# Transposing q and k by DMA instead of on TensorE, in an attention kernel with a maxout FFN behind it

## The chip, the cores and the metric

The kernel runs on one core of a Trainium2 chip. The metric is device time in microseconds. A core has the engines TensorE (PE, matmuls; PEld is its weight load), VectorE (DVE), ScalarE (ACT), GpSimd (POOL) and SyncE (SP), each with its own queue of instructions, and 16 DMA engines that they share. SP and POOL start nearly all transfers of this kernel.

## The reference

Two parts, one behind the other. Attention with a relative position bias, over 8 batches, 8 heads, 576 positions and 64 values per head, and then a feed-forward layer with the maximum of three products:

```python
scores = scale * np.matmul(q, k.transpose(0, 1, 3, 2))         # q, k, v: (8, 8, 576, 64) float32
scores = scores + bias.transpose(2, 0, 1)[None, :, :, :]       # bias[i, j, head] = table[bucket(|i - j|), head]
scores = scores - np.max(scores, axis=-1, keepdims=True)
attn = np.exp(scores)
attn = attn / (np.sum(attn, axis=-1, keepdims=True) + 1e-09)
attn_out = np.matmul(attn, v)
x = attn_out.transpose(0, 2, 1, 3).reshape(B * S, H * D)       # (4608, 512)
h = np.maximum(np.maximum(x @ w1, x @ w2), x @ w3)             # w1, w2, w3: (512, 768)
out = h @ w_out                                                # (4608, 512) float32
```

The bias depends on the distance alone, and from 128 on it is constant, so only a band around the diagonal has to be treated.

## The kernel before

The work goes in pairs of heads: `HP = 4` pairs for each of 8 batches. A pair's two heads of 64 values fill the 128 partitions. q and k are loaded with positions on the partitions, converted from float32 to bf16 by the transfer (`load_q`, `load_k`, issued from POOL), but the score product needs the 64 values of a head on the partitions. So each pair's q and k must be transposed.

Positions 0 to 511 are four blocks of 128 (`KT = 4`) in `batch[b][0]` (q) and `batch[b][1]` (k). The last 64 positions of both heads lie in one more block, in `qtail` and `ktail`, each head in its own half of the partitions and of the columns, with zeros elsewhere. A pair has thus five blocks of 128 x 128 for q and five for k.

`transposes(b, hp)` makes them on PE: ten transposes (through `tr`, line 98) into one PSUM tile `tp` of the pool `ps_s`, which has two buffers that the score tiles use as well, and then two copies by DVE (line 365) into the bf16 tiles `qT` and `kT` in SBUF, two buffers each. It is called once per pair, one pair ahead. Batch 0 has a version of its own, `first_transposes`, which works while the loads are still coming in.

For each pair, the main loop (lines 535 to 569) does this:

- `visit(qT, kT, e4, 0)` (line 397): the scores of all 512 keys against queries 0 to 255, eight matmuls into two tiles `sc`, and the exponentials on ACT (line 395);
- `next_late()`: an `attend` of a pair before. It multiplies the exponentials with v (tile `a`), takes the logarithm of the row sums and the reciprocal by ACT (`ld`, `rd`), and leaves the quotients to DVE, which write them into `xT` (line 462);
- `fill(13, ...)`: some FFN work between, in portions of at most 13 units of PE work; hooks inside it place the quotients and `left_keys`, the last 64 keys;
- `visit(qT, kT, e4, 1)`, the next `attend`, the `transposes` for the pair ahead, another `fill(13, ...)` with `left_queries` (tile `scq`) inside.

`times_band` multiplies the exponentials near the diagonal with the exponentiated bias, on DVE. The FFN (`ffn`) works on chunks of 512 rows, whose portions are spread over a batch's eight fills: products `ps` from `xT` and the weights into the pool `ps_f` (two buffers), a copy by ACT (`m0`), two maxima by DVE (`m`, line 296, and `hT`, line 303), then the output product `pso`, a copy to `osb` (line 316, three buffers) and the store by SP (line 320). Two chunks and the rest of the last one are left for the end, behind the last pair.

PE's order is the program's: every matmul and transpose goes through `inorder`, which places an instruction behind all that was written before it for its engine. The other engines' instructions that have no `inorder` are placed by a planner. Loads for batch b + 2 stand in the last pair of batch b, since they write into the buffer from which batch b's transposes read:

```python
if ahead:
    nxt = transposes(*ahead)
if hp == HP - 1 and b + 2 < B:
    batch[b + 2] = load_tiles()
    load_q(b + 2, 0, H)
    load_k(b + 2, 0, H)
```

The functions that the diff touches:

Of the kernel before, what the change touches and what calls it, by code (L numbers as in the profile page):

```python
# [11 lines left out]
BF16 = mybir.dt.bfloat16  # L12
# [27 lines left out]
def kernel(  # L40
# [12 lines left out]
    nc = tc.nc  # L53
    B, H, S, D = q.shape
    d_model, d_ff = moe_w1.shape
    NB = bias_table.shape[0]
    P = 128
    assert d_model == H * D and S == 576 and D == 64 and NB == 32 and H == 8
    inv_sqrt_d = 1.0 / float(np.sqrt(D))
    HP = H // 2  # L60
# [3 lines left out]
    KT = 4  # L64
# [3 lines left out]
    CH = 512  # L68
# [6 lines left out]
    stage = ctx.enter_context(tc.tile_pool(name="stage", bufs=1))  # L75
    loads = ctx.enter_context(tc.tile_pool(name="loads", bufs=2))
    qkt = ctx.enter_context(tc.tile_pool(name="qkt", bufs=2))
    qk0 = ctx.enter_context(tc.tile_pool(name="qk0", bufs=1))
    ep = ctx.enter_context(tc.tile_pool(name="ep", bufs=3))
    nrm = ctx.enter_context(tc.tile_pool(name="nrm", bufs=3))  # L80
    ffnw = ctx.enter_context(tc.tile_pool(name="ffnw", bufs=2))
# [1 line left out]
    ps_s = ctx.enter_context(tc.tile_pool(name="ps_s", bufs=2, space=bass.MemoryType.PSUM))  # L83
# [8 lines left out]
    inorder = tc.keep_in_program_order  # L92
# [4 lines left out]
    def tr(*args):  # L97
        inorder(nc.tensor.transpose(*args))  # L98
# [22 lines left out]
    def dve_copy(out_, in_):  # L121
        inorder(nc.vector.tensor_copy(out_, in_))
# [20 lines left out]
    def load_main(src, b, h0, h1, dst):  # L143
        x = main_part(src, b)
        if h1 - h0 < KT:
            for h in range(h0, h1):
                nc.gpsimd.dma_start(out=dst[:, :, h, :], in_=x[:, :, h, :])
        else:
            for t in range(KT):
                nc.gpsimd.dma_start(out=dst[:, t, h0:h1, :], in_=x[:, t, h0:h1, :])  # L150
# [5 lines left out]
    def load_tail(src, b, h0, h1, dst):  # L156
        for par in range(2):
            nc.gpsimd.dma_start(  # L158
                out=diag(dst[b % 2], par, h0, h1), in_=tail_part(src, b, h0, h1, par)
            )  # L160

    def load_q(b, h0, h1):
        load_main(q, b, h0, h1, batch[b][0])
        load_tail(q, b, h0, h1, qtail)

    def load_k(b, h0, h1):
        load_main(k, b, h0, h1, batch[b][1])
        load_tail(k, b, h0, h1, ktail)

    def load_v(b, h0, h1):  # L170
        load_main(v, b, h0, h1, vx[b % 2][:].rearrange("p t (h c) -> p t h c", c=P)[:, :, :, 0:D])
        load_tail(v, b, h0, h1, vt)
# [14 lines left out]
    def load_tiles():  # L187
        q_sb = loads.tile([P, KT, H, D], BF16, tag="q_sb", name="q_sb")
        k_sb = loads.tile([P, KT, H, D], BF16, tag="k_sb", name="k_sb")
        return q_sb, k_sb  # L190

    batch = [None] * B
    batch[0] = load_tiles()
    load_k32(0, 2, nc.sync)
    for par in range(2):
# [6 lines left out]
    ident = const.tile([P, P], BF16, name="ident")  # L202
# [7 lines left out]
        out=negc[:], in0=tableT[:, NB - 1 : NB], scalar1=-1.0, scalar2=None, op0=ALU.mult,  # L210
# [40 lines left out]
    def make_band(hp):  # L251
        dve_copy(band[hp][:], hank[:, 2 * hp : 2 * hp + 2, ::-1])
        for par in range(2):
            dve_copy(bandt[hp][64 * par : 64 * par + 64, :], band[hp][0:64, par, 0:192])
# [96 lines left out]
            hook()  # L351


    def transposes(b, hp):
        hs = slice(2 * hp, 2 * hp + 2)
        tp = ps_s.tile([P, 2, 2 * CH], BF16, tag="sc", name="tp")
        made = []
        for j, tl in enumerate((qtail, ktail)):
            for t in range(KT):
                tr(tp[:, j, P * t : P * t + P], batch[b][j][:, t, hs, :].rearrange("p h d -> p (h d)"), ident[:])  # L360
            tr(tp[:, j, KT * P : KT * P + P], tl[b % 2][:, hp, :], ident[:])
        for j in range(2):
            name = ("qT", "kT")[j]
            x = qkt.tile([P, (KT + 1) * P], BF16, tag=name, name=name)
            nc.vector.tensor_copy(x[:], tp[:, j, 0 : (KT + 1) * P])  # L365
            made.append(x)
        return made

    def first_transposes(hp):

        hs = slice(2 * hp, 2 * hp + 2)
        tp = [ps_f.tile([P, 2 * CH], BF16, tag="ff", name=n) for n in ("tq", "tk")]
        made = [qk0.tile([P, (KT + 1) * P], BF16, tag=f"{n}{hp}", name=n) for n in ("qT", "kT")]
        for j in range(2):
            for t in range(KT):
                tr(tp[j][:, P * t : P * t + P], batch[0][j][:, t, hs, :].rearrange("p h d -> p (h d)"), ident[:])
            dve_copy(made[j][:, 0 : KT * P], tp[j][:, 0 : KT * P])

        def tails():
            c = slice(KT * P, KT * P + P)  # L380
            for j, tl in enumerate((qtail, ktail)):
                tr(tp[j][:, c], tl[0][:, hp, :], ident[:])
                dve_copy(made[j][:, c], tp[j][:, c])
        return made, tails
# [12 lines left out]
    def visit(qT, kT, e4, c):  # L397


        for tt in range(0, KT, 2):  # L400
            sc = ps_s.tile([P, 2, 2, QS], F32, tag="sc", name="sc")
            for t in range(2):
                for par in range(2):
                    r = slice(64 * par, 64 * par + 64)
                    mm(
                        sc[:, par, t, :], lhsT=kT[r, P * (tt + t) : P * (tt + t) + P],
                        rhs=qT[r, c * QS : c * QS + QS],
                    )
            exp(e4[:, tt : tt + 2, :, c * QS : c * QS + QS].rearrange("p t h q -> p h t q"), sc[:])
# [60 lines left out]
    def next_late():  # L470
        return late.pop(0)() if late else (lambda: None)

    def e_tiles():
        return (
            ep.tile([P, KT, 2, S], BF16, tag="e4", name="e4"), ep.tile([P, S], BF16, tag="et", name="et")
        )
# [18 lines left out]
    for c, (lo, hi) in enumerate(((0, QS), (QS, S))):  # L495
        for hp in range(HP):
            qT, kT = qk[hp]
            e4, et = e_tiles()
            visit(qT, kT, e4, c)
            if c == 0:  # L500
                if hp == 0:
                    first_tail()
                if hp == 1:
                    dve_copy(batch[0][1][:, :, 4:H, :], k32[:, :, 4:H, :])
                if hp + 1 < HP:
                    main, tail = first_transposes(hp + 1)
                    tail()
                    qk.append(main)

            quotients = next_late() if (c, hp) != (1, 1) else (lambda: None)  # L510
            if c == 0:
                make_band(hp)
                if hp == 1:
                    tail_constants(1)
                    batch[1] = load_tiles()
                    load_q(1, 0, H)
                    load_k(1, 0, H)
            for t in range(KT):
                times_band(hp, e4, t, lo, min(hi, QM))
            if c == 1 and hp == 1:  # L520
                load_v(1, 0, H)
                add_ffn(0, QS)
            if c == 1 and hp == HP - 1:
                nxt = transposes(1, 0)
                batch[2] = load_tiles()
                load_q(2, 0, H)
                load_k(2, 0, H)
            fill(
                12, quotients, lambda: left_keys(hp, qT, kT, et, lo, hi),
                *([lambda: left_queries(qT, kT, e4)] if c == 1 else []),  # L530
            )
            times_band(hp, e4, KT - 1, QM, hi)
            late.append(lambda hp=hp, e4=e4, et=et, lo=lo, hi=hi: attend(0, hp, e4, et, lo, hi))

    pairs = [(b, hp) for b in range(1, B) for hp in range(HP)]
    for i, (b, hp) in enumerate(pairs):
        qT, kT = nxt
        ahead = pairs[i + 1] if i + 1 < len(pairs) else None
        e4, et = e_tiles()

        visit(qT, kT, e4, 0)
        quotients = next_late()
        times_band(hp, e4, 0, 0, QS)
        fill(13, quotients, lambda: left_keys(hp, qT, kT, et, 0, S))


        visit(qT, kT, e4, 1)
        quotients = next_late()  # L550
        times_band(hp, e4, 1, 0, QM)
        times_band(hp, e4, 2, 0, QM)
        if hp == 0:
            if b + 1 < B:
                load_v(b + 1, 0, H)
            if b == 1:
                quotients()
                quotients = lambda: None
            add_ffn(*((QS, QS) if b == 1 else ((b - 1) * CH, CH)))
        if ahead:  # L560
            nxt = transposes(*ahead)
        if hp == HP - 1 and b + 2 < B:
            batch[b + 2] = load_tiles()
            load_q(b + 2, 0, H)
            load_k(b + 2, 0, H)
        fill(13, quotients, lambda: left_queries(qT, kT, e4))
        times_band(hp, e4, 3, 0, S)
        for lo, hi in ((0, QC), (QC, S)):
            late.append(lambda b=b, hp=hp, e4=e4, et=et, lo=lo, hi=hi: attend(b, hp, e4, et, lo, hi))
# [39 lines left out]
```

## Time and profile before

| | us |
|---|---|
| median of 3 runs | 398.64 (398.04 to 399.03) |
| time of the profiled execution | 399.19 |
| its span, from the first to the last instruction | 397.3 |
| PE busy | 353.1 (89%) |
| ACT busy | 277.1 (70%) |
| DVE busy | 263.0 (66%) |
| POOL busy | 115.9 (29%) |
| PEld busy | 199.5 (50%) |

The mean granted clock of PE was 0.996. A row of a timeline gives the start in us from the first instruction, the time until the last of the merged instructions has ended, the engine, the line of the kernel, the operation with what it writes and reads, and the number of instructions merged; a bracket at its end tells how long the engine had stood idle before it, and what ended that. As matmuls overlap in PE's pipeline, a row's duration is more than what it takes of PE's stream. A row on stages gives the busy time of each engine with the number of instructions in brackets, PE's granted clock, the share of the 16 DMA engines in which packets were under way (over 1 where packets overlap) and GB/s. A row on a DMA queue gives packets, MB and the share of 16 engines' span that the packets took. A row on issues gives the number of transfers, KB each, and the median us from issue to landing.

### The profile page before, as it was taken

To read this page: it belongs to the slowest core of one execution; us is meant where nothing else is said; L and a number is where in the kernel's file an instruction comes from. 1 tells how busy PE (TensorE), PEld (TensorE's weight loads), DVE (VectorE), ACT (ScalarE), POOL (GpSimd) and SP (SyncE) were. 2 spreads that over 40 slices of the span, in tenths; PEclk is the share of its full clock that TensorE was granted. 3 is DMA by queue.
4 is the path that set the end of the run, shared out by engine and by line. 5 is a ranking of instruction groups with operands and counts; after the bars stand their busy time and mean duration, and the time that the engine had idled before them with its cause. 6 is when DMAs were issued, how large, how long until landed. Compare 5 with 4: busy or idle time off the path is not lost.

```text
span 397.3 us, 6856 instructions
## 1 busy us (share of the span) xinstructions
PE 353.1 (89%) x2600; PEld 199.5 (50%) x2636; DVE 263.0 (66%) x581; ACT 277.1 (70%) x465; POOL 115.9 (29%) x152
## 2 busy tenths in 40 slices
PE   2396888886899999999999999999999999999995
PEld 1144565554555555555555555545555555444442
DVE  5476556675577767777677767776777677655352
ACT  8249677589588878877888778877886788622221
POOL 8835944035404540263118130904000000000000
PEclk9999999999899999999999999999999999999999
DMA  9999999039904966193809290959000200020202
GB/s 147 199 210 174 132 75 114 0 25 124 75 13 31 91 105 63 11 110 90 77 2 117 86 86 0 96 78 114 0 2 29 79 2 0 28 79 2 106 0 106
DMA packets 121944, 28.56 MB, mean 72 GB/s; under 512 B 113968, under 2 KB 117304, under 8 KB 121912
## 3 DMA queue, kind: packets, MB, share of 16 engines
q0 software_dynamic: 110624, 16.72, 58.3%
q1 hardware_dynamic: 11288, 11.42, 8.8%
q8 instruction: 20, 0.33, 0.3%
q14 instruction: 12, 0.10, 0.1%
HBM read 35.39 MB, written 9.45 MB: 113 GB/s over the span
## 4 chain that ended last, share of the span: by engine, by line
PE 56%; ACT 19%; DVE 15%; issue 5%; DMA 2%; SPq 2%; DVEq 0%
PE ps L95 26%; ACT e L395 15%; PE a L95 12%; PE pso L95 8%; PE sc L95 6%; DVE hT L303 3%; DVE qT L365 3%; DVE xT L462 2%; DVE kT L365 2%; PE sct L95 2%; ACT et L395 2%; DVE e L389 2%; ACT ld L456 1%; DMA w_dr<-w_sb 1%; DMA hank<-w_dr 1%
## 5 line engine op out<-in xcount | busy, mean ns | idle before, releaser
L95 PE MATMUL ps<-xT,w_bf 128*128 128x512 bf16 (+1 forms) x693 | 152.7, 357 | 9.5 <-DVE m L296 3.0
L395 ACT ACTIVATE e<-sc 128x1024 bf16<-128x1024 f32 x128 | 124.0, 1022 | 18.4 <-PE sc L95 17.8
L95 PEld LDWEIGHTS <-w_bf 128*128 128x128 bf16 x720 | 67.8, 98 | 66.1 <-issue 12.2
L389 DVE TENSOR_TENSOR e<-e,band 128x768 bf16<-128x768 bf16 (+4 forms) x140 | 65.9, 478 | 40.5 <-ACT e L395 39.3
L95 PE MATMUL a<-e,vx 128*128 128x288 bf16 (+2 forms) x512 | 76.6, 294 | 0.5 <-DVE e L389 0.5
L462 DVE TENSOR_TENSOR xT<-a,rd 64x288 bf16<-64x288 f32 (+2 forms) x128 | 58.1, 454 | 25.9 <-ACT rd L457 23.9
L277 ACT ACTIVATE m<-ps 128x512 bf16<-128x512 f32 (+1 forms) x60 | 32.9, 548 | 48.3 <-PE ps L95 48.3
L95 PEld LDWEIGHTS <-kT 64*128 64x128 bf16 (+1 forms) x740 | 40.3, 96 | 51.7 <-issue 33.2
L456 ACT ACTIVATE ld<-a 64x288 f32<-64x288 f32 (+2 forms) x128 | 51.9, 406 | 18.6 <-PE a L95 15.4
L95 PEld LDWEIGHTS <-vx 128*128 128x128 bf16 x512 | 45.8, 100 | 27.1 <-issue 16.4
L95 PE MATMUL sc<-qT,kT 64*128 64x256 bf16 x512 | 44.8, 279 | 11.4 <-ACT et L395 6.5
L150 POOL DMA_DIRECT2D q_sb<-in_q_dram x32 | 27.8, 891 | 90.9 <-PE tp L98 89.7
L95 PE MATMUL pso<-wo_bf,hT 128*128 128x512 bf16 x207 | 50.5, 380 | 1.7 <-DVE hT L303 0.5
L296 DVE TENSOR_TENSOR m<-ps,m 128x512 bf16<-128x512 f32 (+1 forms) x60 | 38.3, 638 | 20.7 <-ACT m L277 15.1
L303 DVE TENSOR_TENSOR hT<-ps,m 128x512 bf16<-128x512 f32 (+1 forms) x60 | 38.1, 635 | 17.7 <-PE ps L95 16.0
L95 PEld LDWEIGHTS <-hT 128*128 128x128 bf16 x216 | 20.8, 98 | 26.2 <-DVE hT L303 5.2
L457 ACT ACTIVATE rd<-ld 128x288 f32<-128x288 f32 (+2 forms) x64 | 28.4, 443 | 1.9
L150 POOL DMA_DIRECT2D vx<-in_v_dram x32 | 28.4, 920 | 0.5 <-PE a L95 0.5
L395 ACT ACTIVATE et<-sct 128x576 bf16<-128x576 f32 (+2 forms) x36 | 21.4, 593 | 9.3 <-PE sct L95 9.2
L150 POOL DMA_DIRECT2D k_sb<-in_k_dram x28 | 25.0, 943 | 5.6 <-DMA wo_bf<-in_moe_w_out_dram 2.9
L316 DVE COPY osb<-pso 128x512 f32<-128x512 f32 x32 | 22.0, 689 | 5.4 <-PE pso L95 4.8
L158 POOL DMA_DIRECT2D vt<-in_v_dram x16 | 10.1, 645 | 52.9 <-PE a L95 52.9
(50 smaller groups left out, 229.7 us busy)
## 6 DMA issues: line engine op xcount, KB each, us to landing
out_dram<-osb SPq DMA_DIRECT2D x36, 256.0 KB, 2.0
vx<-in_v_dram POOLq DMA_DIRECT2D x32, 128.0 KB, 4.1
q_sb<-in_q_dram POOLq DMA_DIRECT2D x28, 128.0 KB, 4.0
k_sb<-in_k_dram POOLq DMA_DIRECT2D x28, 128.0 KB, 4.1
w_bf<-in_moe_w_dram POOLq DMA_DIRECT2D x3, 768.0 KB, 12.7
k<-in_k_dram SPq DMA_DIRECT2D x8, 128.0 KB, 3.7
wo_bf<-in_moe_w_out_dram POOLq DMA_DIRECT2D x1, 768.0 KB, 18.8
hank<-w_dr SPq DMA_DIRECT2D x1, 576.0 KB, 7.0
```

The lines of the kernel that those rows point to most:

```text
L95: inorder(nc.tensor.matmul(*args, **kw))
L150: nc.gpsimd.dma_start(out=dst[:, t, h0:h1, :], in_=x[:, t, h0:h1, :])
L277: nc.scalar.activation(out=st[cf]["m0"][:, 0:nt], in_=st[cf]["ps0"], func=ACTF.Copy)
L296: nc.vector.tensor_tensor(out=m[:, 0:nt], in0=st[cf]["ps1"], in1=st[cf]["m0"][:, 0:nt], op=ALU.max)
L303: nc.vector.tensor_tensor(out=hT[:, cf, 0:nt], in0=ps2, in1=st[cf]["m"][:, 0:nt], op=ALU.max)
L316: nc.vector.tensor_copy(osb[:], ps[:])
L365: nc.vector.tensor_copy(x[:], tp[:, j, 0 : (KT + 1) * P])
L389: nc.vector.tensor_tensor(out=e4[:, t, :, lo:hi], in0=e4[:, t, :, lo:hi], in1=band[hp][:, :, lo - P * t + P : hi - P * t + P], op=ALU.mult,)
L395: nc.scalar.activation(out=out_, in_=in_, func=ACTF.Exp, scale=inv_sqrt_d)
L456: nc.scalar.activation(out=ld[r, 0:n], in_=x[par][d, 0:n], func=ACTF.Ln)
L457: nc.scalar.activation(out=rd[:, 0:n], in_=ld[:, 0:n], func=ACTF.Exp, scale=-1.0)
L462: nc.vector.tensor_tensor(out=xT[hp][r, b * S + lo : b * S + hi], in0=x[par][r, 0:n], in1=rd[r, 0:n], op=ALU.mult,)
```

## The change

For batches 1 to 7, the transposes on PE and the copies behind them are replaced by DMA transposes that SP issues. One transfer takes a whole block row, 128 positions by the 512 values of all heads, and writes four 128 x 128 blocks, one for each pair, into tiles `qT` and `kT` that hold a whole batch. A batch has ten: four blocks and the tail, for q and for k. They are issued once per batch, in the second half of the first pair of the batch before (for batch 1: in the last pair of batch 0). The loads of q and k for batch b + 2 move from the last pair of batch b to the first, behind the load of v for batch b + 1. Batch 0 keeps its transposes on PE; they now write into a buffer of the same tiles, and the pool `qk0` goes.

```diff
-    qk0 = ctx.enter_context(tc.tile_pool(name="qk0", bufs=1))
...
-    def transposes(b, hp):
-        hs = slice(2 * hp, 2 * hp + 2)
-        tp = ps_s.tile([P, 2, 2 * CH], BF16, tag="sc", name="tp")
+    def transposes(b):
+
         made = []
         for j, tl in enumerate((qtail, ktail)):
-            for t in range(KT):
-                tr(tp[:, j, P * t : P * t + P], batch[b][j][:, t, hs, :].rearrange("p h d -> p (h d)"), ident[:])
-            tr(tp[:, j, KT * P : KT * P + P], tl[b % 2][:, hp, :], ident[:])
-        for j in range(2):
             name = ("qT", "kT")[j]
-            x = qkt.tile([P, (KT + 1) * P], BF16, tag=name, name=name)
-            nc.vector.tensor_copy(x[:], tp[:, j, 0 : (KT + 1) * P])
+            x = qkt.tile([P, HP, (KT + 1) * P], BF16, tag=name, name=name)
+            for t in range(KT + 1):
+                src = batch[b][j][:, t].rearrange("p h d -> p (h d)") if t < KT else (
+                    tl[b % 2][:].rearrange("p h c -> p (h c)")
+                )
+                inorder(nc.sync.dma_start_transpose(out=x[:, :, P * t : P * t + P], in_=src))
             made.append(x)
         return made
 
+    first_qk = [qkt.tile([P, HP, (KT + 1) * P], BF16, tag=n, name=n) for n in ("qT", "kT")]
+
     def first_transposes(hp):
...
-        made = [qk0.tile([P, (KT + 1) * P], BF16, tag=f"{n}{hp}", name=n) for n in ("qT", "kT")]
+        made = [x[:, hp, :] for x in first_qk]
...
             if c == 1 and hp == HP - 1:
-                nxt = transposes(1, 0)
+                nxt = transposes(1)
                 batch[2] = load_tiles()
...
-    pairs = [(b, hp) for b in range(1, B) for hp in range(HP)]
-    for i, (b, hp) in enumerate(pairs):
-        qT, kT = nxt
-        ahead = pairs[i + 1] if i + 1 < len(pairs) else None
+    for b, hp in [(b, hp) for b in range(1, B) for hp in range(HP)]:
+        if hp == 0:
+            of_batch = nxt
+        qT, kT = (x[:, hp, :] for x in of_batch)
         e4, et = e_tiles()
...
             add_ffn(*((QS, QS) if b == 1 else ((b - 1) * CH, CH)))
-        if ahead:
-            nxt = transposes(*ahead)
-        if hp == HP - 1 and b + 2 < B:
-            batch[b + 2] = load_tiles()
-            load_q(b + 2, 0, H)
-            load_k(b + 2, 0, H)
+            if b + 1 < B:
+                nxt = transposes(b + 1)
+            if b + 2 < B:
+                batch[b + 2] = load_tiles()
+                load_q(b + 2, 0, H)
+                load_k(b + 2, 0, H)
         fill(13, quotients, lambda: left_queries(qT, kT, e4))
```

## The prediction

> **What bounds the kernel now.** I read the page first: busy time, then the chain of work that ended last.
>
> ```profile
> span 397.3 us, 6856 instructions
> ...
> PE 353.1 (89%) x2600; PEld 199.5 (50%) x2636; DVE 263.0 (66%) x581; ACT 277.1 (70%) x465; POOL 115.9 (29%) x152
> ...
> PE 56%; ACT 19%; DVE 15%; issue 5%; DMA 2%; SPq 2%; DVEq 0%
> ```
>
> TensorE (PE) is busy 89% of the span and holds 56% of the chain. But a share is an average over stages, and the change works on seven of eight batches. So next I took the busy times of one whole batch in the middle, from one load of vt to the next:
>
> ```profile
> core 0: us, PE busy (x) PEld busy (x) DVE busy (x) ACT busy (x) POOL busy (x), PEclk, DMA share, GB/s
> 185.53:226.86 41.33, 39.77 (x305) 22.33 (x309) 29.97 (x60) 32.92 (x56) 14.30 (x19) 1.00 0.75 70
> ```
>
> PE works 39.77 of 41.33 us there; ACT, the next, 32.92. PE is the bound, its order is written by hand, and what leaves its stream should shorten the batch as long as ACT and DVE follow. With the 2.2 us less per batch found below, ACT would be busy 32.92 of 39.1 us (84%): still not the bound.
>
> **The change, part by part.**
>
> *1. Ten PE transposes per pair go.* The timeline of one group and of the matmul behind it:
>
> ```profile
> 206.79 0.39 PE L98 MATMUL tp<-ident,q_sb 128*128 128x128 bf16 x4
> 207.01 0.22 PE L98 MATMUL tp<-ident,qtail 128*128 128x128 bf16 x1
> 207.07 0.39 PE L98 MATMUL tp<-ident,k_sb 128*128 128x128 bf16 x4
> 207.29 0.22 PE L98 MATMUL tp<-ident,ktail 128*128 128x128 bf16 x1
> 207.35 1.03 PE L95 MATMUL ps<-xT,w_bf 128*128 128x512 bf16 x4
> ```
>
> The 0.22 us of one transpose is the wrong price, since matmuls overlap in the pipeline: the ten hold the stream for 207.35 - 206.79 = 0.56 us. The rows of the tile tp give the number of groups, 112 / 4 = 28, and the sum over the span gives their busy time as a union (second row: PE, then DVE):
>
> ```profile
> L98 PE MATMUL tp<-ident,q_sb x112: 219/219/311, 50.2 to 330.9; 128*128 128x128 bf16 x112
> ```
> ```profile
> 0.00:397.00 397.00, 20.75 (x280) 24.82 (x56) 1.00 0.67 72
> ```
>
> 28 x 0.56 = 15.7 us. From above, 20.75 us: that union also holds, behind each group, the last transpose's end in the pipeline (20.75 / 28 - 0.56 = 0.18 us), which overlaps the next matmul. I take 15.7, which is per batch 4 x 0.56 = 2.2 us.
>
> *2. Two DVE copies per pair go* (24.82 us of DVE in all). DVE is not the bound, so most of this costs and gains nothing; but the copies stand ahead of work that PE waits for. The second half of one pair:
>
> ```profile
> 198.03 0.48 DVE L365 COPY qT<-tp 128x640 bf16<-128x640 bf16 x1
> 198.41 0.44 ACT L457 ACTIVATE rd<-ld 128x288 f32<-128x288 f32 x1
> 198.43 0.48 DVE L365 COPY kT<-tp 128x640 bf16<-128x640 bf16 x1
> 198.83 0.68 DVE L303 TENSOR_TENSOR hT<-ps,m 128x512 bf16<-128x512 f32 x1
> 199.09 0.39 PE L95 MATMUL scq<-qT,kT 128*128 128x128 bf16 x4
> 199.29 0.60 ACT L277 ACTIVATE m<-ps 128x512 bf16<-128x512 f32 x1 [0.43 <-PE ps L95]
> 199.43 0.93 DVE L462 TENSOR_TENSOR xT<-a,rd 64x288 bf16<-64x288 f32 x2
> 199.56 1.02 PE L95 MATMUL ps<-xT,w_bf 128*128 128x512 bf16 x4
> ```
>
> The last product starts at 199.56, just after hT ended (198.83 + 0.68 = 199.51), since hT frees its bank of the two in ps_f; hT in turn stood behind the two copies. PE's four scq matmuls, at the transposes' spacing of 0.056 us, were issued by 199.31, so PE lost 0.25 us there. Without the copies hT can start when the product before it is ready, some 0.7 us earlier, and this wait mostly goes: 0 to 0.25 us for the 21 pairs with hp 1 to 3. I take 0.1 x 21 = 2 us.
>
> In the pairs with hp 0 the bank is freed by another copy:
>
> ```profile
> 187.88 0.92 DVE L462 TENSOR_TENSOR xT<-a,rd 64x288 bf16<-64x288 f32 x2
> ...
> 188.83 0.69 DVE L316 COPY osb<-pso 128x512 f32<-128x512 f32 x1
> ...
> 189.55 0.33 SPq L320 DMA_DIRECT2D out_dram<-osb  x1
> 189.58 1.02 PE L95 MATMUL ps<-xT,w_bf 128*128 128x512 bf16 x4
> ```
>
> Here the product at 189.58 waits for osb (ends 189.52), which stands behind xT, and xT starts when ACT's rd is done, a time the transposes don't set. If DVE keeps that order, the 0.56 us are lost again to this wait; if osb goes first they are kept. Seven such pairs: 0 to 3.9 us given back. The order can fall either way, so I take the middle, 2 us.
>
> *3. Ten transfers per batch are added on SP*, each 128 x 512 bf16 (128 KB), 70 in all. The trace has no crossbar transpose, so their price is bounded by neighbours:
>
> ```profile
> q0 software_dynamic: 110624, 16.72, 58.3%
> q1 hardware_dynamic: 11288, 11.42, 8.8%
> ```
> ```profile
> k_sb<-in_k_dram POOLq DMA_DIRECT2D x28, 128.0 KB, 4.1
> ```
>
> Packet time on the software queue: 0.583 x 397.3 x 16 / 110624 = 33.5 ns; on the hardware queue 0.088 x 397.3 x 16 / 11288 = 49.6 ns. Cut into rows of 256 bytes, a transfer is 512 packets: 512 x 33.5 / 16 = 1.07 us, or 1.59 us at 49.6. If instead each began only when the one before had landed, 4.1 us, as the load of the same 128 KB takes. An element at a time (65,536 packets) it would be 137 us, which I take as excluded in practice, since the kernel would need over 9 ms. I take 1.6 us, from the nearer row (the hardware queue); ten are 16 us.
>
> *When are they due?* For batch b+1 they stand in SP's order behind the stores of the first half of pair (b,0), and the next batch's scores need the first nine:
>
> ```profile
> 179.77 5.52 SPq L320 DMA_DIRECT2D out_dram<-osb  x3
> ```
> ```profile
> 220.09 0.39 PE L95 MATMUL sc<-qT,kT 64*128 64x256 bf16 x4
> ```
>
> From 179.77 + 5.52 = 185.29 to 220.09, less the 2.2 us that the batch gets shorter, are 32.6 us. Nine take 14.4 us at my price, 36.9 us at 4.1. So they are hidden with 18 us to spare; the cover is gone at 32.6 / 9 = 3.6 us each. Behind them on SP stands one store (189.55 above), late by up to 16 us; the next comes at 179.77 + 41.33 = 221.1, 31 us later, and osb has three buffers, so nobody waits. If that cover fails, osb, then its bank, then PE wait.
>
> *4. The loads of q and k for batch b+2 move* from (b,3) to (b,0), right behind v's. Before, POOL stood waiting:
>
> ```profile
> 207.47 3.50 POOL L150 DMA_DIRECT2D q_sb<-in_q_dram  x4 [17.19 <-PE tp L98]
> ```
>
> Now they start about 17 us earlier, in the same stretch as the ten transposes. Twelve transfers behind six of v make POOL issue for its 14.30 us in one go. Packets: 0.75 x 41.33 = 31 us of loads and 11 to 16 us of transposes, 42 to 47 us in all. The highest share in the trace,
>
> ```profile
> 20.00:40.00 20.00, 15.95 (x113) 9.26 (x112) 14.57 (x47) 14.25 (x27) 8.32 (x11) 1.00 1.57 191
> ```
>
> is 1.57 (overlapping packets count twice), which would clear everything in 27 to 30 us, even then inside 32.6. The loads are needed a batch later: cost 0.
>
> *5. Batch 1's transfers* need k's load, and pair (1,0)'s scores need them:
>
> ```profile
> 38.10 1.27 POOL L158 DMA_DIRECT2D ktail<-in_k_dram  x2 [0.31 <-issue]
> ```
> ```profile
> 55.43 0.76 PE L95 MATMUL sc<-qT,kT 64*128 64x256 bf16 x8
> ```
>
> k lands by about 38.1 + 4.1 = 42.2; five of k at 1.6 us end at 50.2, against 54.9 (55.43 - 0.56): cost 0, with 5 us to spare; at 4.1 us kT's fourth block would be 3.7 us late.
>
> *6. New waits on PE.* Each batch's first matmuls wait for ten transfers instead of two copies. A satisfied wait has no row; at most one slot of PE's stream each (0.056 us, the spacing above) makes 70 x 0.056 = 3.9 us, at least 0. I take 1 us, nearer the bottom, since the group above shows PE passing from transposes to products, with waits of their own, without a gap.
>
> **Sum.** -15.7 - 2 + 2 + 1 = -14.7 us. The profiled execution took 399.19 us, 0.55 over the median of the runs (398.64), so 398.64 - 14.7 = 383.9; forecast 384 us, 3.7% less. Its own bounds: best -20.75 - 5.3 = 372.6 (every term at its end; unlikely together), plainly -15.7 - 2 = 381; worst with transfers on time -15.7 + 3.9 + 3.9 = 390.7. Own range 379 to 391.
>
> **Rivals.**
>
> *A, slower: the transfers are late.* Place: the first scores of each batch. If transfers run one behind another's landing at 4.1 us, the ninth comes 36.9 - 32.6 = 4.3 us late in six batches (26 us) and 3.7 us late in batch 1; with the 14.7 saved, 398.6 - 14.7 + 29.7 = 413.6 us. It decides from 32.6 / 9 + 14.7 / 6 / 9 = 3.9 us per transfer. For it: k_sb's 4.1 us, and that loads are in flight in the same stretch. Against: transfers on a queue overlap in this trace; POOL issued four loads of q_sb in 3.50 us, less than one such load's 4.1 us to landing. The Trainium skill, "VectorE: DVE Perf Modes", section "The three transpose paths", lists 1,309 ns for a 128 x 128 bf16 block by the DMA crossbar beside 390 ns on TensorE. No run here shows the first, and the second is far above the 56 ns spacing measured here, so these look like times of one block alone; as an estimate from that page, four blocks in series would be 5.2 us a transfer and the kernel about 476 us. "Advanced Engine Details and Errata", section "X-Bar Transpose (TRN2)", of the same Trainium skill says against it that such transfers are as fast as regular ones; by that, my price holds.
>
> *B, the gain is given back on DVE and ACT.* The bank waits of part 2 stay in most pairs: each group's 0.56 us turns into a longer wait for hT or osb. With all seven hp 0 pairs and half of the other 21 lost, 15.7 x 17.5 / 28 = 9.8 us go and no wait is saved: 398.6 - 5.9 + 1 = 393.7. For it: the two places above. Against: in 21 pairs the releaser itself moves up, since it stood behind the removed copies.
>
> *C, no change:* all 28 given back, 398.6 us. For it only that ACT's 84% leaves 1.5 us of slack in a pair; against, PE's 39.77 of 41.33.
>
> **How the numbers follow.** What a measurement of this kernel can tell from no change is about 0.3%, 1.2 us. Forecast's case 0.64; B 0.14; C 0.05; A 0.14, any worse price included; above the forecast's gain (under 379) 0.03. Faster: 0.64 + 0.14 + 0.03 = 0.81; same 0.05; slower 0.14. The range 379 to 395 holds the forecast's case and most of B, about 0.78; it leaves out A, C and the best ends.
>
> **What would show it.** Right: no tp rows, 280 PE matmuls and 56 copies fewer; the batch (vt load to vt load) at about 39 us; PE still over 95% busy in it; transposes landing some 15 us before the next batch's first sc. Step 2: the product behind scq no longer starts at hT's end; in hp 0 pairs, whether osb stands before xT. Wrong by A: PE sc or PEld waiting on DMA qT or kT, once per batch; by B: more idle time before ps, on DVE hT, DVE osb or ACT m, with ACT over 85% busy. Also wrong if the loads of v or the one store are held up by the transposes so long that PE a waits on DMA vx or vt, or PE pso on DVE osb.

## The result and the profile after

The changed kernel takes 383.0 us (median of four runs, 382.9 to 384.6) against 398.6 us before: ratio 0.962, 95% interval 0.959 to 0.965, so 15.5 us less. The forecast was 384. The profiled execution took 384.6 us, 1.6 us more than the other three runs, and it has a stretch of lower granted clock (mean 0.991, the others 1.000).

The page of the changed kernel, busy time and chain:

```profile
span 382.9 us, 6399 instructions
...
PE 336.2 (88%) x2323; PEld 182.9 (48%) x2356; DVE 241.1 (63%) x525; ACT 275.6 (72%) x465; POOL 116.1 (30%) x152
...
PE 62%; ACT 18%; DVE 9%; DMA 5%; issue 4%; SPq 1%; DVEq 0%
```

PE lost 16.9 us of busy time and DVE 21.9, and the span 14.4. DVE's share of the chain fell from 15% to 9%, a hint that the copies had counted for more than the forecast gave them; they are priced below. DMA's share rose from 2% to 5%; what is new is the last transfer of kT for batch 1, with 2.1%.

Three whole batches, from load of vt to load of vt (columns as before):

```profile
141.52:181.01 39.49, 37.14 (x266) 20.01 (x269) 26.98 (x52) 32.66 (x56) 14.27 (x18) 1.00 1.08 106
181.01:220.49 39.48, 37.09 (x265) 20.00 (x269) 26.97 (x52) 32.66 (x56) 14.30 (x18) 1.00 1.08 106
220.49:259.04 38.55, 37.15 (x266) 20.05 (x269) 26.97 (x52) 32.66 (x56) 4.75 (x6) 1.00 0.64 78
```

41.33 us have become 39.5 in the earlier and 38.55 in the later batches, and PE is still busy 94 to 96% of them. The two lengths are one finding, explained below. The transfers show up as DMA share, 0.75 before and 1.08 now (0.64 in the third row, where no loads of q and k are left).

What a transfer costs SP (ns, minimum/median/maximum) and when it lands, for qT's blocks, then the queues:

```profile
L363 SPq DMA_TRANSPOSE qT<-q_sb x28: 1197/1230/2291, 37.0 to 262.6; - x28
...
DMA to landing us min/median/max: 2.4/5.1/9.5
```
```profile
q0 software_dynamic: 110624, 16.72, 68.2%
q1 hardware_dynamic: 49368, 20.60, 25.4%
...
q_sb<-in_q_dram POOLq DMA_DIRECT2D x28, 128.0 KB, 7.2
```

The hardware queue has 49368 - 11288 = 38,080 more packets, 544 a transfer. Its packet time grew from 0.088 x 397.3 x 16 = 559 us to 0.254 x 382.9 x 16 = 1,556, so a transfer is 997 / 70 / 16 = 0.89 us of all 16 engines, if the stores' own packets take as long as before, and SP spends 1.23 us on it. The loads pay: a load of q lands after 7.2 us instead of 4.0, and the same 110,624 packets of the software queue take 68.2% instead of 58.3%.

They still land early enough. SP's timeline around one batch's k, and the next batch's first scores (start and duration in us):

```profile
188.24 5.18 SPq L363 DMA_TRANSPOSE kT<-k_sb  x4
...
194.88 0.53 SPq L319 DMA_DIRECT2D out_dram<-osb  x1
```
```profile
213.51 0.39 PE L94 MATMUL sc<-qT,kT 64*128 64x256 bf16 x4
```

The last k block is issued by 193.4, and with the longest landing seen (9.5 us) it is there at 203, ten before it is needed. The store behind the transfers left 10 us after its osb was ready, and nobody waited for it.

### The profile page after: what moved, and what is told of

Same layout as the page of the kernel before. It is cut to its first block, busy times and chain, and to the rows that moved or that the text cites. A ratio compares the mean times of both kernels' runs of the same rounds, so it can differ in the third digit from the quotient of the medians.

```text
span 382.9 us, 6399 instructions
## 1 busy us (share of the span) xinstructions
PE 336.2 (88%) x2323; PEld 182.9 (48%) x2356; DVE 241.1 (63%) x525; ACT 275.6 (72%) x465; POOL 116.1 (30%) x152
## 3 DMA queue, kind: packets, MB, share of 16 engines
q0 software_dynamic: 110624, 16.72, 68.2%
q1 hardware_dynamic: 49368, 20.60, 25.4%
## 4 chain that ended last, share of the span: by engine, by line
PE 62%; ACT 18%; DVE 9%; DMA 5%; issue 4%; SPq 1%; DVEq 0%
PE ps L94 31%; PE a L94 14%; ACT e L395 9%; PE pso L94 7%; PE sc L94 6%; ACT ld L456 3%; DVE xT L462 3%; ACT rd L457 2%; DVE osb L315 2%; DMA kT<-k_sb 2%; PE sct L94 2%; DVE e L389 2%; ACT et L395 1%; DMA hank<-w_dr 1%; DMA w_dr<-w_sb 1%
## 5 line engine op out<-in xcount | busy, mean ns | idle before, releaser
L462 DVE TENSOR_TENSOR xT<-a,rd 64x288 bf16<-64x288 f32 (+2 forms) x128 | 58.3, 455 | 33.8 <-ACT rd L457 22.5
L456 ACT ACTIVATE ld<-a 64x288 f32<-64x288 f32 (+2 forms) x128 | 51.8, 405 | 18.7 <-PE a L94 15.3
L94 PE MATMUL pso<-wo_bf,hT 128*128 128x512 bf16 x207 | 49.6, 379 | 1.0 <-DVE hT L302 0.5
L315 DVE COPY osb<-pso 128x512 f32<-128x512 f32 x32 | 21.9, 686 | 5.3 <-PE pso L94 4.8
```

The source lines that it names most:

```text
L94: inorder(nc.tensor.matmul(*args, **kw))
L315: nc.vector.tensor_copy(osb[:], ps[:])
L456: nc.scalar.activation(out=ld[r, 0:n], in_=x[par][d, 0:n], func=ACTF.Ln)
L462: nc.vector.tensor_tensor(out=xT[hp][r, b * S + lo : b * S + hi], in0=x[par][r, 0:n], in1=rd[r, 0:n], op=ALU.mult,)
```

## The experiments

### PE's work or DVE's copies put back (e1_pe_back, e2_pe_dve_back, e3_dve_only)

```diff
+    def on_pe(b, hp):                     # e1, e2: the ten transposes of before, into tp
+        tp = ps_s.tile([P, 2, 2 * CH], BF16, tag="sc", name="tp")
+        ... tr(tp[...], ...) x10
+        ... nc.vector.tensor_copy(y[:], tp[:, j, 0 : (KT + 1) * P])   # e2 only, twice
...
+        on_pe(min(b + 1, B - 1), (hp + 1) % HP)
         fill(13, quotients, lambda: left_queries(qT, kT, e4))
```
```diff
+            for j in range(2):            # e3: two DVE multiplications instead
+                inorder(nc.vector.tensor_tensor(out=y[:], in0=qT, in1=kT, op=ALU.mult))
         fill(13, quotients, lambda: left_queries(qT, kT, e4))
```

Expected of e1_pe_back:

> The changed kernel, and besides its DMA transposes the ten PE transposes of each pair stand again at their old place in PE's order; their result in PSUM is read by nobody, and the two DVE copies do not come back. The scores use what the DMA transposes made. Theory (the gain is the stream slot of 0.56 us in 28 groups plus some waits behind the copies): 28 x 0.56 = 15.7 us come back in part, since without copies the banks are free earlier: 383.0 + 10 to 14 = 393 to 397 us. Rival (PE's slot was slack, and the gain came from the DVE copies): under 387 us.

Expected of e2_pe_dve_back:

> As the kernel before with the DMA transposes added: PE transposes and the two DVE copies per pair are back, the copies go into a tile that nobody reads, and the scores use what the DMA transposes made. Against the kernel before, this prices the 70 transfers with their contention, queues and the late start of batch 1. Theory (the transfers are hidden but for batch 1, where PE waited 1.9 us for kT): 398.6 + 1 to 3 = 399.6 to 401.6 us. Rival (the transfers cost PE or its partners a few us in every batch, and the gain would be larger without them): over 404 us.

Expected of e3_dve_only:

> The changed kernel with two DVE multiplications of 128 x 640 bf16 per pair (0.49 us each, as long as a copy of before) where the copies stood, into a tile that nobody reads; no PE transposes. Theory (copies ahead of hT lengthen a bank wait by 0.2 to 0.4 us in the pairs with hp 1 to 3): 383.0 + 4 to 8 = 387 to 391 us. Rival (DVE has slack, only PE's slot counts): 383 to 384.5 us.

Measured: e1 405.9 us, e2 415.0, e3 391.0. Both numbers with PE's transposes lie far above the theory; by e2 the transfers would cost 16 us. Before taking that, I looked at who waited: in e2, PE waits 12.0 us for hT ahead of ps, in the kernel before 0.4. The second half of a pair in e1 shows why (DVE and PE rows, those of ACT, SP and the band left out):

```profile
288.52 0.45 DVE L470 TENSOR_TENSOR xT<-a,rd 64x288 bf16<-64x288 f32 x1 [0.78 <-ACT rd L465]
...
288.90 0.67 DVE L302 TENSOR_TENSOR hT<-ps,m 128x512 bf16<-128x512 f32 x1
...
289.60 0.46 DVE L470 TENSOR_TENSOR xT<-a,rd 64x288 bf16<-64x288 f32 x1
289.62 1.02 PE L94 MATMUL ps<-xT,w_bf 128*128 128x512 bf16 x4 [0.51 <-DVE hT L302]
```

The planner has put one xT ahead of hT here, and hT waits for a result of ACT that it doesn't need. In the kernel before, hT came first. So e1 and e2 changed DVE's order besides what they were meant to change, and they tell nothing of the transfers. e3 agrees with its theory at the upper end: two operations as long as the copies cost 7.9 us. In its trace, though, hT stands between the two in the second half of a pair, so it is not quite the order of before.

### The same with DVE's order held (p_before, p_both, p_pe, p_after)

DVE's instructions of batches 1 to 7 go through `inorder`, in all four alike: p_before is the kernel before, p_both has the DMA transposes besides, p_pe has no copies, p_after has no PE transposes either.

```diff
+    def dv(ins):
+        return inorder(ins) if pinned[0] else ins        # pinned in batches 1 to 7
...
-            nc.vector.tensor_tensor(out=hT[:, cf, 0:nt], ...)
+            dv(nc.vector.tensor_tensor(out=hT[:, cf, 0:nt], ...))   # also m, osb, band, et, xT and the copies
```

Expected of p_before:

> The kernel before, with DVE's instructions of batches 1 to 7 held in the order in which the program writes them (hT, then both xT, in the second halves; osb before xT in the pairs with hp 0). The planner's own order in the kernel before is the same but for osb, so both theories expect 398.6 us, within 2.5 us. It is the base for the next three, which hold the same order.

Expected of p_both:

> The kernel before plus the DMA transposes (PE transposes and DVE copies stay, the copies go into a tile that nobody reads, the scores use the DMA's result), DVE's order held as in p_before. Theory (the 16 us of e2_pe_dve_back over the kernel before came from the planner, which put one xT ahead of hT; the transfers are hidden but for batch 1): p_before + 0.5 to 3 us, with pairs of batches 3 to 7 as long as in p_before. Rival (the transfers themselves slow the engines or the loads): p_before + 10 us or more.

Expected of p_pe:

> As p_both without the two DVE copies per pair; DVE's order held. p_both minus this is the copies' share. Theory: 5 to 9 us under p_both (bank waits behind hT of 0.2 to 0.4 us in most pairs). Rival (copies fall into DVE's slack): within 1 us of p_both.

Expected of p_after:

> The changed kernel with DVE's order held as in p_before. p_pe minus this is the share of PE's slot: theory 28 x 0.56 = 15.7 us, 11 to 16 with what turns into waits; rival (slack on PE) under 5 us. Against the changed kernel: the second xT no longer stands behind osb in the pairs (2,0) to (4,0), where PE waited 1.2 us for it, so 0.5 to 2 us faster, 381 to 382.5 us, if osb ahead of both xT does not cost the same.

Measured: 404.2, 408.5, 401.9 and 387.1 us. The held order is itself 4 to 5.6 us slower than the planner's (404.2 against 398.6, 387.1 against 383.0): it sets the maximum m ahead of the last band multiplication of a pair, where it waits for PE. So the two expectations that compared with the planner's kernels were wrong. Among themselves the four are comparable, best in a batch without disturbance: scq of pair (6,0) and of (7,0), p_before, p_both, p_pe and p_after in turn:

```profile
276.05 0.39 PE L99 MATMUL scq<-qT,kT 128*128 128x128 bf16 x4
...
317.71 0.39 PE L99 MATMUL scq<-qT,kT 128*128 128x128 bf16 x4
```
```profile
280.41 0.39 PE L99 MATMUL scq<-qT,kT 128*128 128x128 bf16 x4
...
322.46 0.39 PE L99 MATMUL scq<-qT,kT 128*128 128x128 bf16 x4
```
```profile
276.85 0.39 PE L98 MATMUL scq<-qT,kT 128*128 128x128 bf16 x4
...
317.75 0.39 PE L98 MATMUL scq<-qT,kT 128*128 128x128 bf16 x4
```
```profile
263.54 0.39 PE L98 MATMUL scq<-qT,kT 128*128 128x128 bf16 x4
...
302.50 0.39 PE L98 MATMUL scq<-qT,kT 128*128 128x128 bf16 x4
```

That is 41.66, 42.05, 40.90 and 38.96 us for a batch.

- *PE's slot* (p_pe to p_after): 1.94 us a batch, 13.6 in seven; by the medians 14.9, but these also hold batch 1, whose first pair is 3.4 us longer in p_pe's profile. Forecast 2.24 and 15.7. The pairs with hp 1 to 3 gain 0.51 to 0.55 us each, those with hp 0 only 0.33.
- *The copies* (p_before to p_pe, whose DMA transposes cost this batch next to nothing): 0.76 us a batch, 5.3 in seven: nothing in hp 0 and hp 1, 0.24 in hp 2, 0.52 in hp 3. Forecast 2. The comparison that was set up for it, p_both to p_pe, gives 1.15 a batch and 6.6 by the medians, inside the 5 to 9 expected, but p_both has a fault of its own (next point).
- *The transfers* (p_before to p_both): 0.39 us a batch, but not where they run. They are in flight in the pairs with hp 0 and hp 1, and the marks of those pairs are 10.44 and 10.01 us apart, in p_before 10.43 and 10.01. The 0.39 fall into hp 2 and hp 3. I put them down to the two copies, which no longer overlap, since in p_both both write one tile (first row p_both, then p_before); PE's waits for hT, which stands behind them, rise from 0.9 to 5.1 us over the span:

```profile
299.75 1.01 DVE L381 COPY y<-tp 128x640 bf16<-128x640 bf16 x2
```
```profile
295.25 0.48 DVE L369 COPY qT<-tp 128x640 bf16<-128x640 bf16 x1
295.65 0.48 DVE L369 COPY kT<-tp 128x640 bf16<-128x640 bf16 x1
```

So in a batch behind the first the transfers cost nothing that the trace shows. p_both's median lies 4.4 us above p_before, above the 3 of the theory and far below the 10 of the rival. Of these, 7 x 0.39 = 2.7 are this fault of the experiment; 1 us is lost ahead of pair (1,0), and the rest falls into batch 1, where p_both's profile has a stretch of lower clock.

### The moved loads (e4_loads_back)

```diff
-            if b + 2 < B:
+        if hp == HP - 1 and b + 2 < B:
             batch[b + 2] = load_tiles()
```

> The changed kernel, with the loads of q and k for batch b + 2 back in the last pair of batch b. Theory (the moved loads gain nothing and cost nothing; the transposes of the next batch start later because they wait for these loads, but still land in time): 383 us, within 1.5 us. Rival (loads and transposes in one stretch hurt each other on the path): 1.5 to 4 us faster than the changed kernel. Other rival (late loads make the transposes late): over 386 us.

Measured: 383.7 us, within 1 us of the changed kernel (383.0). But the edit moved the loads in the program only. POOL's order is the planner's, and its loads of q start within 1 us of those in the changed kernel (first two rows e4_loads_back, then the changed kernel):

```profile
152.38 3.51 POOL L149 DMA_DIRECT2D q_sb<-in_q_dram  x4 [6.25 <-DMA qT<-q_sb]
...
191.39 3.50 POOL L149 DMA_DIRECT2D q_sb<-in_q_dram  x4 [5.78 <-DMA qT<-q_sb]
```
```profile
153.37 3.50 POOL L149 DMA_DIRECT2D q_sb<-in_q_dram  x4 [7.10 <-DMA qT<-q_sb]
...
191.81 3.51 POOL L149 DMA_DIRECT2D q_sb<-in_q_dram  x4 [6.05 <-DMA qT<-q_sb]
```

So this run does not test the move, although its time is the one expected.

### The lead (l_late)

```diff
-            if b + 1 < B:                 # in the pair (b,0)
+        if hp == 2 and b + 1 < B:
             nxt = transposes(b + 1)
```

> The changed kernel with the ten transfers for the next batch issued in the pair (b,2) instead of (b,0), some 12 us before the next batch's first scores. SP needs 1.3 us for each, and the last landed 4 to 5 us after its issue, so the ninth comes 9 x 1.3 + 4.5 = 16 us after the first. Theory (a transfer is paid only where it lands late): 2 to 5 us late in each of six batches, 395 to 413 us, with PE waiting on DMA kT. Rival (the transfers run one behind another's landing, 4 us each): 24 us late per batch, over 500 us. Rival (the lead does not matter): 383 us.

Measured: 384.1 us, and the transfers hardly moved:

```profile
183.43 0.33 SPq L319 DMA_DIRECT2D out_dram<-osb  x1
183.86 1.23 SPq L363 DMA_TRANSPOSE qT<-q_sb  x1
```

In the changed kernel the first transfer of this batch stands at 180.65. The place in the program says only what stands ahead of an instruction in its own queue. SP has nothing there but the store of pair (b,0), and the transfers wait for nothing of pair (b,2); they start as soon as that store is gone. My expectation took the place for a time. How late the transfers may come, and so rival A's threshold of 3.9 us, was not tried.

### Order by need, and both xT ahead of osb (n_need, x_quot, b_both)

```diff
+        by_need = [(0, 0), (0, 1), (1, 0), (1, 1), (1, 2), (1, 3), (0, 2), (0, 3), (1, 4), (0, 4)]
+        for j, t in by_need:              # n_need: j = 0 for q, 1 for k
...
+        pinned[0] = hp == 0 and 2 <= b <= 4   # x_quot: xT, xT, osb through inorder
+        if pinned[0]:
+            quotients()
+            quotients = lambda: None
         fill(13, quotients, lambda: left_queries(qT, kT, e4))
```

Expected of n_need:

> The changed kernel with the ten transfers of a batch in the order in which they are needed: two of q, four of k, two of q, the tails. Theory (batch 1 starts late because kT's blocks stand behind five of q): the 1.9 us of PE's wait on kT shrink by 1 to 2 us, 381 to 382 us; the other batches are unchanged. Rival (k's load lands so late that the order does not matter, or the delay is made up later): within 0.5 us of the changed kernel.

Expected of x_quot:

> The changed kernel with DVE's order held in the pairs (2,0) to (4,0): both xT, then osb. There the first FFN product reads the rows that these xT write, and PE waited 1.2 us for the second xT behind osb. Theory: 0.4 to 0.7 us per pair, 1.2 to 2 us in all, 381 to 382 us. Rival (the later osb holds the next product as long): within 0.5 us of the changed kernel.

Expected of b_both:

> Both edits, order by need and both xT ahead of osb. Theory: the two gains add, 379 to 381.5 us. Rival: as the better of the two alone.

Measured: 383.2, 382.7 and 384.2 us. None differs from the changed kernel by more than the runs scatter (382.9 to 384.6), so no time gained is shown. The nearest to one is x_quot: its two runs with a mean clock of 1.000 took 381.5 and 382.2 us, the three of the changed kernel 382.9 to 383.0.

At its place each edit did what it should. In the changed kernel PE stood twice at the first scores of batch 1:

```profile
55.56 0.28 PE L94 MATMUL sc<-qT,kT 64*128 64x256 bf16 x2 [0.93 <-DMA kT<-k_sb]
...
56.86 0.28 PE L94 MATMUL sc<-qT,kT 64*128 64x256 bf16 x2 [1.01 <-DMA kT<-k_sb]
```

In n_need the eight run through, and from the scq ahead of them to the next are 9.99 us instead of 12.1:

```profile
54.28 0.39 PE L94 MATMUL scq<-qT,kT 128*128 128x128 bf16 x4
54.50 0.60 PE L94 MATMUL ps<-xT,w_bf 128*128 128x256 bf16 x4
55.04 0.76 PE L94 MATMUL sc<-qT,kT 64*128 64x256 bf16 x8
```

x_quot shortens the pairs (3,0) and (4,0) from 11.46 to 10.85 us and lengthens the next from 9.18 to 9.46, 0.33 us net each. Pair (2,0) keeps its 11.3: there the planner of the changed kernel had both xT ahead of osb already. Profile against profile, b_both is 3.4 us shorter from its first scq to its last (290.8 us against 294.2), but only 2.0 over the whole (382.6 against 384.6). Part of the 3.4 (pair (2,0), 10.18 against 11.34) lies where the changed kernel's profile has its stretch of lower clock. Its four runs had granted clocks of 0.990 to 0.996, while three of the four of the changed kernel had 1.000. Whether the lower clock follows from the denser stream stays open, and with it whether the edits are worth anything.

## Why the prediction was right, point by point

The forecast (384 us, range 379 to 395) held: 15.5 us were measured, 14.7 forecast. Part of that is luck: the slot was forecast 2.1 us too large and batch 1 at nothing instead of 1.9, the copies 3.3 too small, and these errors cancel.

**1, PE's slot: right.** 15.7 forecast; 13.6 by the undisturbed batch, 14.9 by the medians. What is missing lies mostly in the hp 0 pairs. Pricing by the start of the next matmul was the step that mattered: by the duration of one transpose, 280 x 0.22 us, it would have been 62.

**2, the copies: right mechanism, undersized.** 2 us forecast, 5.3 measured (e3's operations of the same length cost 7.9). The wait behind hT is gone, as said:

```profile
193.84 0.68 DVE L302 TENSOR_TENSOR hT<-ps,m 128x512 bf16<-128x512 f32 x1
...
194.35 0.39 PE L94 MATMUL scq<-qT,kT 128*128 128x128 bf16 x4
194.58 1.02 PE L94 MATMUL ps<-xT,w_bf 128*128 128x512 bf16 x4
```

hT ends at 194.52, and ps starts 0.23 us after scq, the time of four matmuls. I took 0.1 us for this in 21 pairs. The whole visible gap of 0.25 us would have given 5.2, the right sum, but not the right places: in the held order hp 1 gains nothing, hp 2 the gap and hp 3 twice as much. Why is open.

**2, the hp 0 pairs: about the right sum, by another wait.** I feared that osb behind xT would hold the next product's bank, and gave back 2 us over seven pairs. That wait did not grow. It is found in (5,0) to (7,0), 0.26 us each where it was 0.31, and these pairs take 10.10 us instead of 10.44, so they keep 0.34 of the slot's 0.56:

```profile
223.94 0.81 PE L94 MATMUL ps<-xT,w_bf 128*128 128x512 bf16 x3 [0.26 <-DVE osb L315]
```

But (3,0) and (4,0) are longer than before, 11.46 us against 10.62, and the wait there is another one:

```profile
183.73 0.67 DVE L315 COPY osb<-pso 128x512 f32<-128x512 f32 x1
184.44 0.46 DVE L462 TENSOR_TENSOR xT<-a,rd 64x288 bf16<-64x288 f32 x1
184.95 0.38 PE L94 MATMUL ps<-xT,w_bf 128*128 128x512 bf16 x1 [1.19 <-DVE xT L462]
```

PE's product stops at its last quarter, the one that reads xT of hp 3. The planner now put osb between the two xT, and the chunk begun in (b,0) ends at row 512 b, while the second half of hp 3's quotients starts at row 576 (b - 1) + 288: they overlap for b up to 4, and not from 5 on. That is a true dependence on data, which I had missed in the code; x_quot, which sets osb behind, takes 0.61 us off these pairs. In (2,0) the rows overlap too, but both xT stand ahead of osb, as they did before, and PE does not wait. The dependence explains the two batch lengths. Price: 2 x (0.84 + 0.34) = 2.4 us against what the later batches gain.

**3, the transfers: right.** 1.6 us each forecast, 1.23 us of SP and 0.89 of packets measured. Hidden in batches 2 to 7, by some nine us at least, even with the longest landing. The Trainium skill ("Advanced Engine Details and Errata", section "X-Bar Transpose (TRN2)") has such transfers as fast as regular ones, and the trace agrees: 997 us of packet time, summed over the engines, by 38,080 packets is 26 ns a packet, less than the 33.5 of the loads before. The 1,309 ns that the Trainium skill ("VectorE: DVE Perf Modes", section "The three transpose paths") gives for one block is close to SP's 1.23 us for a whole transfer of four.

**4, the loads: cost right, times wrong.** I had them start about 17 us earlier, beside the transposes. Counted through the kernel, the rows at 153.37 and 191.81 above are the loads of q for batches 6 and 7, issued in batches 3 and 4. Batch 6's came 21.9 us behind the load of v for batch 5 before (207.47 and 185.53) and comes 27.6 us ahead of it now (153.37 and 181.01), some 50 us earlier: the planner has moved it past that load in POOL's queue. It overwrites the q of batch 4 and so has to wait for the DMA transposes of that batch, whose q blocks SP had issued by 146.4. That is the wait in the brackets, 9.8, 7.1 and 6.1 us in batches 2 to 4. No cost of the loads is seen: the pairs (4,1) to (4,3), with loads of q and k issued among them, take 9.18, 9.19 and 9.65 us, and (6,1) to (6,3), with none, 9.60, 9.19 and 9.66.

**5, batch 1: wrong.** Forecast: hidden with 5 us to spare. Measured: PE waits 1.9 us. Two steps failed. The smaller is the start: I let five transfers of k begin when k's load had landed, at 42.2, and did not reckon with q's five ahead of them in SP's queue. q's load stands behind the weights and landed 18.7 to 20.3 us after its issue (18.9 at worst in the kernel before; the only landing I had taken was 4.1, the median of k's loads), so SP could not start before

```profile
36.99 5.40 SPq L363 DMA_TRANSPOSE qT<-q_sb  x4
...
43.99 6.29 SPq L363 DMA_TRANSPOSE kT<-k_sb  x4
```

The larger is the landing of the transfers themselves, for which I had no term: I took a block as there when SP's 1.6 us for it were over. Here, among the loads of batch 2, kT's blocks landed 8.0 to 8.5 us after their issue. The last was issued at 48.83 and landed at 56.8, where PE's second wait ends. n_need shows that the order decides here.

**6, new waits on PE: nothing.** I had taken 1 us; the pairs with hp 0 and 1 of p_both and p_before agree to 0.01 us.

Together: -13.6 - 5.3 + 2.4 + 1.9 = -14.6, against -14.4 between the two spans. That is closer than the parts are known: the first two are prices of one undisturbed batch with a held order, times seven, and stretches of lower clock and other moves of the planner lie in both spans. Rival A happened in batch 1 alone, at 1.9 us. Rival B happened in two pairs, by another wait than it named. Rival C did not.

## What to carry to other kernels

Work that leaves the bounding engine is worth the slot up to its neighbour's start, and copies on an engine that isn't the bound are worth the bank waits behind them: look what stands behind each removed instruction in its own queue. For a transfer that must land by a certain time, take the slowest landing of its stretch, not the median, and order several by need. When an edit is meant to move an instruction, look in the trace when it starts now: two edits here (l_late, e4_loads_back) hardly moved anything. When an experiment lets a planner reorder another engine, compare the orders before believing the time.

## What the runs showed of the hardware that I had not expected

- A DMA transpose of 128 x 512 bf16 holds SP for about 1.2 us (median of 28, the longest 2.3), while its landing goes from 2.4 to 9.5 us.
- In some runs the granted clock falls for a few us: to 0.50 between 95 and 100 us in the profile of the changed kernel, to 0.83 between 100 and 110 us before. Three runs of the changed kernel had a mean clock of 1.000 and took 383.0 us, the profiled one 0.991 and 384.6. Pair (2,0), in which the fall lies, takes 11.34 us there and 10.13 in l_late, whose clock is 1.00 from 90 to 115 us. Why it falls in one run and not in another stays open. The row of this stretch, with the columns of the table of batches above (the granted clock is third from the end):

```profile
95.00:100.00 5.00, 4.36 (x21) 2.01 (x20) 1.83 (x4) 3.53 (x7) 0.00 (x0) 0.50 0.41 79
```
